# First-layer weight tiles from every fourth column, w_out in 8 KB rows, and w_in in three loads

## The chip, the cores and the metric

The kernel runs on one core of one Trainium2 chip. The core has five engines that run side by side: TensorE (PE in the profile, with its weight loads as PEld), VectorE (DVE), ScalarE (ACT), GpSimd (POOL) and SyncE (SP). Transfers between the chip's memory and the core's are issued here by SP and by POOL and carried out by the core's 16 DMA engines. The metric is the device time of one execution in microseconds; lower is better. Before the change the median of three runs is 308.4 us (308.37 to 308.42).

## The reference

Two steps follow each other. The first is attention with a window: 8 batches, 8 heads, 576 positions of 64 numbers, each position looking at those at most 32 away.

```python
scores = 1/sqrt(64) * q @ k.T                 # for each batch and head
scores = where(abs(i - j) <= 32, scores, -1e9)
attn   = exp(scores - max) / (sum + 1e-9)
x      = (attn @ v), heads side by side       # 4608 tokens x 512
```

The second is a layer pair on all 4608 tokens, with w_in of 512 x 2048 and w_out of 2048 x 512:

```python
h = x @ w_in
g = maximum(0.01 * h, h)
out = g @ w_out                               # 4608 x 512, float32
```

All inputs are float32; the kernel multiplies in bf16.

## The kernel before, in words

**Attention.** The work is cut into steps, one for a pair of heads and a stretch of tokens. In a step PE multiplies keys with queries (`score`, L429), ACT takes the exponential, POOL or DVE multiplies by the mask, PE forms the row sums (`row_sums`, L467) and the product with v (`product`, L517), and DVE inverts the sums and scales (`scaled`, L541), which leaves x transposed in `xT`: 128 rows (two heads) for each of four pairs p. Batches 0 and 1 are loaded plainly (`load_qk`, L68, on SP's queue), cast to bf16 (`cast_qk`, L286; the engines for q and k are its arguments) and transposed on PE (`transposes`, L327, matmuls at L340 and L344); later batches are transposed by the DMA engines.

**First layer.** The tokens are cut into groups `GROUPS` (L557), 288 tokens each for the first four. For a group g the first layer makes 16 tiles, f = 0 to 15; tile f is the product of columns 128 f to 128 f + 127 of w_in with xT, four matmuls that add up over the 512 inputs in chunks c of 128 (`h_mms`, L564, matmul at L567). The columns of w_in are the weights that PE loads ahead of each matmul. ACT applies the leaky ReLU and writes `gT[:, f]` (L572). w_in stands in one tile, `w_in_bf`, and is loaded by `load_w_in(f0, f1)` (L726) from POOL's queue, which also casts it to bf16: four loads of 512 columns, so that the weights of tiles 4 i to 4 i + 3 come with load i. A row of such a load is 512 floats, 2 KB, and there are 128 x 4 rows.

**Second layer.** For 128 tokens, 16 matmuls add up over the tiles f (L637; L653 in the first pair of output tiles, `o_pair`, L645, which goes through w_out in parts of four tiles f: (0,0), (0,1), (0,2), (1,0), and so on). `load_w_out(i)` (L729) brings rows 512 i to 512 i + 511 of w_out, again on POOL's queue with a cast: `w_out_bf[p, 4 i + c]` holds row 512 i + 128 c + p, so a row of the load is one row of w_out, 2 KB, and there are 128 x 4.

**Order.** The order is written out by hand; each engine takes its instructions in the order of the program, and an instruction that waits holds back those behind it on its engine. The part around the change is L733 to L860: the loads of w_in stand on POOL between casts and masks (L750, L767, L768, L785), those of w_out at L798, L804, L805 and L823. `h_first(0)` (L613) is a generator that makes tiles 0 to 3 of group 0 chunk by chunk: its first step takes four PSUM buffers, each further one issues the four matmuls of one chunk c, which needs the pair c of xT. Those steps stand between the attention work of steps 3 to 5 (L787 to L802). Then come tiles 4 to 15 of group 0 with the rest of the attention of batch 0 between them (L814), and group 1 (L846 to L859), into which `second_pair(p)` (L827) puts the transposes of batch 1, pair p, after tiles 7 and 11; pairs 2 and 3 come within `o_pair`. The q of batch 1 is cast on DVE, the k on POOL (L831, L838, L840, L859); on POOL the order is k of pair 0, two small clears, k of pair 1, three loads of v, a part of the band mask, k of pair 2, three loads of v, a mask, k of pair 3. The loads of q and k of batch 1 are issued on SP at L797, released by a one-element write on POOL (L75).

`row_sums_by_quarters(3)` (L485) makes the row sums of step 3 in another layout, with its matmuls at L490; `spread(3)` (L498) brings the inverse back.

The functions that the change touches, and those that call them:

Of the kernel before, what the change touches and what calls it, by code (L numbers as in the profile page):

```python
# [10 lines left out]
BF16 = mybir.dt.bfloat16  # L11
# [5 lines left out]
def kernel(  # L17
# [15 lines left out]
    nc = tc.nc  # L33
# [5 lines left out]
    DFF = moe_w_in.shape[1]  # L39
# [4 lines left out]
    DMC = DMODEL // 128  # L44
# [4 lines left out]
    const = ctx.enter_context(tc.tile_pool(name="const", bufs=1))  # L49
# [154 lines left out]
    for lo in (0, 64):  # L204
        w = win[lo:lo + 64]
        nc.gpsimd.affine_select(
            out=w, in_=w, compare_op=ALU.is_ge, fill=0.0,
# [3 lines left out]
            out=w, in_=w, compare_op=ALU.is_ge, fill=0.0,  # L211
# [53 lines left out]
    def clear_k(i, eng=nc.gpsimd):  # L265
# [7 lines left out]
        out=ps[:, 512:512 + HALF], in_=zero.to_broadcast([128, HALF]), func=AF.Copy,  # L273
# [4 lines left out]
    NEW_RING = 1024  # L278
    OLD = 8 * BY_DMA
    xT = const.tile([128, NPAIR, RING], BF16)  # L280
    w_in_bf = const.tile([128, DMC, DFF], BF16)
    w_out_bf = const.tile([128, FFC, DMODEL], BF16)

    def cast_qk(b, p, q_eng=nc.gpsimd, k_eng=nc.gpsimd):  # L286
        for eng, src, dst in ((q_eng, qf, qb), (k_eng, kf, kb)):
            if eng is None:
                continue
            if b == 0:  # L290
                to, tok = dst[:, p, 0:NB * D], src[b, p]
            else:
                to = dst[0:96, p].rearrange("p (c a d) -> p c a d", a=2, d=D)
                tok = src[b, p].rearrange("p a (c d) -> p c a d", d=D)
            if eng is nc.scalar:
                eng.activation(out=to, in_=tok, func=AF.Copy)
            else:
                eng.tensor_copy(out=to, in_=tok)  # L298
# [77 lines left out]
    def where(i):  # L376
        return i // 8, (i // 4) % 2, i % 4
# [6 lines left out]
    def score_blocks(i):  # L384
        p, bs = i % NPAIR, blocks_of(i)
        n = 2 * 64 * len(bs)
        lo = 512 * (i % 2)
        sc = ps[:, lo:lo + n].rearrange("p (a w c i) -> p a w c i", a=2, c=2, i=32)
        for w, (b, m) in enumerate(bs):
            tok = qz[b % 2][:, p, m // 3].rearrange("p a (c i) -> p a c i", c=2)  # L390
            at = 32 * (m % 3)
            nc.tensor.matmul(  # L392
                sc[:, :, w], kz[b % 2][:, p, 64 * m:64 * m + 128],
                tok[:, :, :, at:at + 32], start=True, stop=True,
            )
        e = attn.tile([128, 2 * HALF], BF16, name="e")
        nc.scalar.activation(out=e[:, 0:n], in_=ps[:, lo:lo + n], func=AF.Exp, scale=scale)  # L397
        pr = prob[:, i % NPROB].rearrange("p n i -> p (n i)")[:, 0:n]
        nc.gpsimd.tensor_mul(pr, e[:, 0:n], band.rearrange("p w c i -> p (w c i)")[:, 0:n])  # L399
        probs[i] = pr.rearrange("p (a w i) -> p a w i", a=2, i=64)  # L400
# [28 lines left out]
    def score(i, masked_by=nc.gpsimd):  # L429
        if i >= OLD:  # L430
            return score_blocks(i)
        b, hf, p = where(i)
        tok = qT[b][:, p, hf * HALF:hf * HALF + HALF]
        if b == 0:

            for a, n_, m in ((0, 0, 0), (1, 1, 0), (0, 0, 1), (1, 1, 1), (0, 0, 2),
                             (0, 1, 0), (1, 0, 0), (0, 1, 1), (1, 0, 1), (1, 0, 2)):
                blk, i0, n = WIN[hf][n_][m]
                r = slice(64 * a, 64 * a + 64)
                nc.tensor.matmul(  # L440
                    ps_v[r, n_, i0:i0 + n], first_keys[p][r, 64 * blk:64 * blk + 64],
                    tok[r, i0:i0 + n], start=True, stop=True,
                )
        else:
            for n_, blocks in enumerate(WIN[hf]):
                for blk, i0, n in blocks:
                    nc.tensor.matmul(  # L447
                        ps_v[:, n_, i0:i0 + n], kbd[b % 2][:, p, blk],
                        tok[:, i0:i0 + n], start=True, stop=True,
                    )  # L450
        e = attn.tile([128, 2 * HALF], BF16, name="e")
        nc.scalar.activation(out=e, in_=ps[:, P0:P0 + 2 * HALF], func=AF.Exp, scale=scale)  # L452
        pr = prob[:, i % NPROB]
        masked_by.tensor_mul(  # L454
            pr.rearrange("p n i -> p (n i)"), e, mask[hf].rearrange("p n i -> p (n i)"),
        )
        probs[i] = [pr, None, None]
# [27 lines left out]
    def row_sums_by_quarters(i):  # L485
        s = xps.tile([128, 512], FP32, name="s")
        pr = probs[i][0]
        for j in range(4):
            for n in range(2):
                nc.tensor.matmul(  # L490
                    s[:, 0:QUART], to_rows[:, 96 - 32 * j:224 - 32 * j],
                    pr[:, n, QUART * j:QUART * j + QUART],
                    start=(j == 0 and n == 0), stop=(j == 3 and n == 1),
                )
        nc.vector.reciprocal(quarters, s[:, 0:QUART])
        probs[i][2] = s

    def spread(i):  # L498
        s = probs[i][2]
        for j in range(4):  # L500
            nc.tensor.matmul(
                s[:, 128 + QUART * j:128 + QUART * j + QUART], from_rows[:, 128 * j:128 * j + 128],
                quarters, start=True, stop=True,
            )
        probs[i][2] = s[:, 128:128 + HALF]
# [6 lines left out]
    def sums(i):  # L512
        if probs[i][2] is None:
            row_sums(i)
            inverse(i)

    def product(i):  # L517

        b, hf, p = where(i)
        pr = probs[i][0]  # L520
        x = xps.tile([128, 512], FP32, name="x")[:, 0:HALF]
        parts = [(n_, *block) for n_ in range(2) for block in WIN[hf][n_]]
        for n_, blk, i0, n in parts:
            nc.tensor.matmul(  # L524
                x[:, i0:i0 + n], vbd[b % 2][:, p, blk, :], pr[:, n_, i0:i0 + n],
                start=(blk == parts[0][1]), stop=(blk == parts[-1][1]), skip_group_check=True,
            )
        if i in (1, 2, 3):

            to = kept[i] if i < 3 else recip.tile([128, HALF], FP32, name="r")  # L530
            nc.scalar.activation(out=to, in_=x, func=AF.Copy)
            x = to
        probs[i][1] = x
# [7 lines left out]
    def scaled(i):  # L541
        _, x, r = probs.pop(i)
        nc.vector.tensor_mul(place(i), x, r)
# [14 lines left out]
    t0, new = 0, NTOK - BY_DMA * S  # L558
    while t0 < new:
        n = 256 if t0 < 2048 else min(512, new - t0)  # L560
# [3 lines left out]
    def h_mms(g, f, h, cs):  # L564
        t0, n = GROUPS[g]
        for c in cs:
            nc.tensor.matmul(  # L567
                h[:, 0:n], w_in_bf[:, c, ts(f, 128)], xT[:, c, t0:t0 + n],
                start=(c == 0), stop=(c == DMC - 1),
            )  # L570

    def h_out(g, f, h):  # L572
        t0, n = GROUPS[g]
        to, h = gT[:, f, t0:t0 + n], h[:, 0:n]
        nc.scalar.activation(out=to, in_=h, func=AF.Prelu, alpha=0.01)  # L575
# [37 lines left out]
    def h_first(g):  # L613

        hs = [mmps.tile([128, 512], FP32, name="mm", tag="mm") for _ in range(4)]
        yield hs[0]
        for c in range(DMC):
            for f in range(4):
                h_mms(g, f, hs[f], (c,))
            if c == DMC - 1:  # L620
                for f in range(4):
                    h_out(g, f, hs[f])
            yield
# [38 lines left out]
    def warm_up(n, w=512):  # L662
        t = xps.tile([128, 512], FP32, name="x")
        for _ in range(n):
            nc.tensor.matmul(
                t[:, 0:w], idle[:, 0:128], idle[:, 0:w], start=True, stop=True,
                skip_group_check=True,
            )
# [52 lines left out]
        state["done"] += 1  # L721

    w_in_r = moe_w_in.rearrange("(c p) f -> p c f", p=128)
    w_out_r = moe_w_out.rearrange("(c p) f -> p c f", p=128)

    def load_w_in(f0, f1):  # L726
        nc.gpsimd.dma_start(out=w_in_bf[:, :, f0:f1], in_=w_in_r[:, :, f0:f1])  # L727

    def load_w_out(i):  # L729
        c = slice(4 * i, 4 * i + 4)  # L730
        nc.gpsimd.dma_start(out=w_out_bf[:, c, :], in_=w_out_r[:, c, :])

    first = transposes(0)  # L733

# [27 lines left out]
    next(first)  # L762
    next(first)
    warm_up(2)
    cast_qk(0, 3, nc.scalar, nc.gpsimd)
    load_cast_v(0, 3, (1,))
    load_w_in(512, 1024)  # L767
    load_w_in(1024, 1536)  # L768
    sums(1)
    score(2, masked_by=nc.vector)  # L770
    next(first)
# [7 lines left out]
    product(1)  # L779
    score(4)  # L780
    product(2)
    row_sums_by_quarters(3)
    scaled(1)
    scaled(2)
    load_w_in(1536, 2048)  # L785
    clear_on_act(kbd[1][:, 1])
    h0 = h_first(0)  # L787
    h = next(h0)
    next(h0)
    product(3)  # L790
    score(5)
    spread(3)
    scaled(3)
    next(h0)
# [79 lines left out]
    at, t = {1: 0.0}, 0.0  # L874
# [93 lines left out]
```

## Time and profile before

| | |
|---|---|
| median of the runs | 308.4 us (308.37, 308.40, 308.42) |
| the profiled execution | 308.76 us |
| its span, first to last instruction | 307.1 us |
| PE busy | 298.0 us, 97% |
| PEld, weight loads beside PE | 193.5 us, 63% |
| DVE, ACT, POOL busy | 72%, 66%, 66% |
| granted TensorE clock, mean | 1.000 |
| moved by the DMA engines | 48.31 MB in 121506 packets |

The profile is that of one execution. A span of an engine is the time in which it was busy; PEld overlaps PE. A row of the timeline gives start, duration, engine, line, operation, tiles and shape, and in brackets the idle time of the engine just before with what released it. The DMA view counts packets by queue: q0 is fed by POOL, q1 by SP. A load is split over the 16 DMA engines and has landed when the last of them is through.

### The profile page before, as it was taken

The numbers are of one execution on the slowest core, as the hardware profiler recorded it, in microseconds if no ns is written. First come the engines' busy times: TensorE is split into PE (matmuls) and PEld (weight loads), VectorE is DVE, ScalarE is ACT, GpSimd is POOL, SyncE is SP. The second block draws the span as 40 slices with busy tenths as digits, with TensorE's granted clock in tenths as the row PEclk, the third lists the DMA queues.
The fourth block names the chain that finished last, engine by engine and source line by source line (L and its number), as shares of the span: only waits on it lengthen the run. The fifth ranks groups of instructions, "written<-read, shape, count | busy, mean of one in ns | idle before, by whom it ended". The sixth has DMA issues, their size and how long they took to land.

```text
span 307.1 us, 6942 instructions
## 1 busy us (share of the span) xinstructions
PE 298.0 (97%) x2616; PEld 193.5 (63%) x2646; DVE 221.7 (72%) x302; ACT 204.1 (66%) x423; POOL 201.5 (66%) x258
## 2 busy tenths in 40 slices
PE   8799999999999999999999999999999999999996
PEld 3577855676757777676768685858555555444643
DVE  6879579597888987897799777898689766743000
ACT  7876964564946677685858585849589548843731
POOL 8989799867999996889577366579757533110000
PEclk9999999999999999999999999999999999999999
DMA  7999999998999999999969984994950110001002
GB/s 248 205 183 268 264 152 218 218 209 145 208 186 215 191 256 188 190 192 228 208 151 237 226 177 113 204 204 106 196 121 1 36 68 36 0 34 72 34 31 74
DMA packets 121506, 48.31 MB, mean 157 GB/s; under 512 B 96256, under 2 KB 115968, under 8 KB 121472
## 3 DMA queue, kind: packets, MB, share of 16 engines
q1 hardware_dynamic: 107776, 42.48, 67.9%
q0 software_dynamic: 13696, 5.38, 14.5%
q8 instruction: 21, 0.34, 0.5%
q14 instruction: 13, 0.11, 0.1%
HBM read 36.70 MB, written 9.44 MB: 150 GB/s over the span
## 4 chain that ended last, share of the span: by engine, by line
PE 86%; DMA 6%; POOL 5%; issue 1%; ACT 1%; POOLq 0%; ACTq 0%
PE mm L637 38%; PE mm L567 36%; DMA w_out_bf<-in_moe_w_out_dram 6%; PE ps L392 4%; PE s L410 2%; POOL set L147 2%; PE x L410 2%; PE mm L653 2%; POOL w_in_bf L727 1%; PE x L524 1%; POOL prob L454 1%; PE ps L447 0%; POOL kb L298 0%; ACT gT L575 0%; PE s L479 0%
## 5 line engine op out<-in xcount | busy, mean ns | idle before, releaser
L567 PE MATMUL mm<-xT,w_in_bf 128*128 128x256 bf16 (+3 forms) x956 | 133.5, 294 | 0.2
L637 PE MATMUL mm<-w_out_bf,gT 128*128 128x512 bf16 (+2 forms) x537 | 122.5, 373 | 1.3
L419 DVE RECIPROCAL r<-r 128x256 f32<-128x256 f32 (+1 forms) x56 | 95.0, 1696 | 34.3 <-ACT r L418 33.7
L567 PEld LDWEIGHTS <-w_in_bf 128*128 128x128 bf16 x960 | 91.4, 98 | 29.6
L399 POOL TENSOR_TENSOR prob<-e,band 128x512 bf16<-128x512 bf16 (+1 forms) x56 | 62.6, 1118 | 56.8 <-ACT e L397 55.6
L637 PEld LDWEIGHTS <-gT 128*128 128x128 bf16 x560 | 52.1, 98 | 54.1
L575 ACT ACTIVATE gT<-mm 128x288 bf16<-128x288 f32 (+2 forms) x112 | 49.9, 479 | 12.4 <-PE mm L567 9.9
L397 ACT ACTIVATE e<-ps 128x512 bf16<-128x512 f32 (+1 forms) x56 | 32.4, 579 | 27.6 <-PE ps L392 24.6
L642 ACT ACTIVATE o_sb<-mm 128x512 f32<-128x512 f32 (+2 forms) x35 | 20.5, 585 | 39.2 <-PE mm L637 38.9
L598 ACT ACTIVATE gT<-mm 128x512 bf16<-128x512 f32 x64 | 35.7, 596 | 5.3 <-PE mm L567 3.9
L509 DVE RECIPROCAL r<-s 128x288 f32<-128x288 f32 x13 | 25.4, 1957 | 3.8 <-PE s L476 2.4
L423 DVE TENSOR_TENSOR xT<-x,r 64x256 bf16<-64x256 f32 (+1 forms) x56 | 24.4, 436 | 3.7 <-PE mm L567 0.5
L298 POOL CAST kb<-kf 96x768 bf16<-96x768 f32 (+1 forms) x30 | 25.0, 832 | 3.0 <-DMA kf<-in_k_dram 2.5
L423 DVE TENSOR_TENSOR xT<-s,r 64x256 bf16<-64x256 f32 (+1 forms) x56 | 24.4, 435 | 3.3
L324 DVE COPY set<-kT 64x576 bf16<-64x576 bf16 x48 | 21.4, 446 | 1.7 <-DMA kT<-qb 0.8
L392 PEld LDWEIGHTS <-set 128*128 128x128 bf16 x216 | 16.8, 98 | 9.2
L392 PE MATMUL ps<-set 128*128 128x128 bf16 x216 | 21.2, 219 | 0.0
L303 POOL CAST set<-vbuf 128x640 bf16<-128x640 f32 x24 | 17.2, 717 | 4.5 <-DMA vbuf<-in_v_dram 2.8
L298 POOL CAST qb<-qf 96x768 bf16<-96x768 f32 x24 | 19.7, 820 | 0.1
L454 POOL TENSOR_TENSOR prob<-e,mask 128x576 bf16<-128x576 bf16 x13 | 16.5, 1275 | 2.9 <-ACT e L452 2.8
L410 PEld LDWEIGHTS <-set 128*128 128x128 bf16 x432 | 18.0, 98 | 0.5
L304 POOL CAST set<-vbuf 64x512 bf16<-64x512 f32 x24 | 14.6, 610 | 1.5
(104 smaller groups left out, 242.2 us busy)
## 6 DMA issues: line engine op xcount, KB each, us to landing
qf<-in_q_dram SPq DMA_DIRECT2D x32, 288.0 KB, 5.5
kf<-in_k_dram SPq DMA_DIRECT2D x32, 288.0 KB, 6.1
out_dram<-o_sb SPq DMA_DIRECT2D x35, 256.0 KB, 2.9
vbuf<-in_v_dram SPq DMA_DIRECT2D x15, 256.0 KB, 4.6
w_in_bf<-in_moe_w_in_dram POOLq DMA_DIRECT2D x4, 512.0 KB, 8.4
w_out_bf<-in_moe_w_out_dram POOLq DMA_DIRECT2D x4, 512.0 KB, 15.6
vbuf<-in_v_dram SPq DMA_DIRECT2D x10, 192.0 KB, 4.4
set<-in_v_dram POOLq DMA_DIRECT2D x16, 72.0 KB, 6.4
```

The source lines that it names most:

```text
L298: eng.tensor_copy(out=to, in_=tok)
L392: nc.tensor.matmul(sc[:, :, w], kz[b % 2][:, p, 64 * m:64 * m + 128], tok[:, :, :, at:at + 32], start=True, stop=True,)
L397: nc.scalar.activation(out=e[:, 0:n], in_=ps[:, lo:lo + n], func=AF.Exp, scale=scale)
L399: nc.gpsimd.tensor_mul(pr, e[:, 0:n], band.rearrange("p w c i -> p (w c i)")[:, 0:n])
L410: nc.tensor.matmul(x[:, a, w], vw[b % 2][:, p, m, a:a + 2].rearrange("p n d -> p (n d)"), pr[:, a, w], start=True, stop=True,)
L419: nc.vector.reciprocal(r[:, 0:n], r[:, 0:n])
L423: nc.vector.tensor_mul(xT[rows, p, t0:t0 + n].rearrange("p (w i c) -> p w c i", i=32, c=2), x[rows, a].rearrange("p (w c i) -> p w c i", c ...
L509: nc.vector.reciprocal(r, probs[i][2])
L567: nc.tensor.matmul(h[:, 0:n], w_in_bf[:, c, ts(f, 128)], xT[:, c, t0:t0 + n], start=(c == 0), stop=(c == DMC - 1),)
L575: nc.scalar.activation(out=to, in_=h, func=AF.Prelu, alpha=0.01)
L598: nc.scalar.activation(out=gT[:, f - 1:f + 1, t0:t0 + 256], in_=hh.rearrange("p (f t) -> p f t", f=2), func=AF.Prelu, alpha=0.01,)
L637: nc.tensor.matmul(o[:, lo:hi], gT[:, f, t0:t0 + 128], w_out_bf[:, f, lo:hi], start=(f == 0), stop=(f == FFC - 1),)
```

## The change

- A tile f of the first layer takes every fourth column: within a block of 512 columns n, tile 4 n + j takes columns 512 n + j, 512 n + j + 4, and so on, 128 of them. The weights of a matmul are then read with a step of four elements.
- To match that, `w_out_bf[p, 4 i + c]` holds row 512 i + 4 p + c, so that partition p takes four neighbouring rows of w_out, 8 KB in one piece, and a load has 128 rows in place of 512.
- w_in stands in three tiles of 512, 512 and 1024 columns. The third load brings the last 1024 columns at once, in rows of 4 KB; it stands where the load of columns 1024 to 1535 stood. The load at L785 goes. Tiles 8 to 15 now read the third tile.
- `h_first(0)` is begun earlier: its buffers and the first three matmuls of chunk 0 come before `row_sums_by_quarters(3)`; the fourth comes after `score(5)`.
- The cast of q, batch 0, pair 3, goes from ACT to DVE, where it stands behind the mask of step 1.

```diff
-    w_in_bf = const.tile([128, DMC, DFF], BF16)
+    w_in_parts = [const.tile([128, DMC, n], BF16, name=f"w_in{n_}") for n_, n in enumerate((512, 512, 1024))]
     w_out_bf = const.tile([128, FFC, DMODEL], BF16)
+
+    def w_in_cols(c, f):
+        n = min(f // 4, 2)
+        at = 128 * (f - 4 * n - f % 4)
+        return w_in_parts[n][:, c, at + f % 4:at + 512:4]
...
-                h[:, 0:n], w_in_bf[:, c, ts(f, 128)], xT[:, c, t0:t0 + n],
+                h[:, 0:n], w_in_cols(c, f), xT[:, c, t0:t0 + n],
...
             for f in range(4):
+                if c == 0 and f == 3:
+                    yield
                 h_mms(g, f, hs[f], (c,))
...
-    w_out_r = moe_w_out.rearrange("(c p) f -> p c f", p=128)
+    w_out_r = moe_w_out.rearrange("(i p c) f -> p i c f", p=128, c=4)
 
     def load_w_in(f0, f1):
-        nc.gpsimd.dma_start(out=w_in_bf[:, :, f0:f1], in_=w_in_r[:, :, f0:f1])
+        nc.gpsimd.dma_start(out=w_in_parts[min(f0 // 512, 2)], in_=w_in_r[:, :, f0:f1])
 
     def load_w_out(i):
         c = slice(4 * i, 4 * i + 4)
-        nc.gpsimd.dma_start(out=w_out_bf[:, c, :], in_=w_out_r[:, c, :])
+        nc.gpsimd.dma_start(out=w_out_bf[:, c, :], in_=w_out_r[:, i])
...
-    cast_qk(0, 3, nc.scalar, nc.gpsimd)
+    cast_qk(0, 3, nc.vector, nc.gpsimd)
     load_cast_v(0, 3, (1,))
     load_w_in(512, 1024)
-    load_w_in(1024, 1536)
+    load_w_in(1024, 2048)
...
     product(2)
+    h0 = h_first(0)
+    next(h0)
+    next(h0)
     row_sums_by_quarters(3)
     scaled(1)
     scaled(2)
-    load_w_in(1536, 2048)
     clear_on_act(kbd[1][:, 1])
-    h0 = h_first(0)
-    h = next(h0)
-    next(h0)
     product(3)
     score(5)
+    next(h0)
     spread(3)
     scaled(3)
     next(h0)
```

## The prediction, made before the run

> **What bounds the kernel now.** I read the page first: the share of each engine says which one the span hangs on.
>
> ```profile
> PE 298.0 (97%) x2616; PEld 193.5 (63%) x2646; DVE 221.7 (72%) x302; ACT 204.1 (66%) x423; POOL 201.5 (66%) x258
> ```
>
> PE is busy 97% of a span of 307.1 us, so what keeps PE waiting comes straight out of the time, and little waiting is left. The view of who waited for whom, for PE alone, shows what the change could remove:
>
> ```profile
> PE mm L653 <- DMA w_out_bf<-in_moe_w_out_dram: 0.6, 1, 0.6
> PE s L490 <- POOL prob L454: 0.6, 1, 0.6
> ```
>
> Columns are us in total, times, longest. Both are single waits of 0.6 us. The timeline of PE gives their places, and three places more that the change touches (start, duration, then in brackets the idle time before):
>
> ```profile
> 16.67 0.42 PE L490 MATMUL s<-prob,set 128*128 128x72 bf16 x8 [0.58 <-POOL prob L454]
> ...
> 24.44 0.65 PE L567 MATMUL mm<-xT,w_in_bf 128*128 128x288 bf16 x4
> ...
> 36.06 0.42 PE L344 MATMUL tp<-ident,kb 96*128 96x96 bf16 x6
> ...
> 38.77 0.42 PE L344 MATMUL tp<-ident,kb 96*128 96x96 bf16 x6
> ...
> 41.74 1.89 PE L653 MATMUL mm<-w_out_bf,gT 128*128 128x512 bf16 x8 [0.59 <-DMA w_out_bf<-in_moe_w_out_dram]
> ```
>
> The row at 24.44 is tile f=8 of the first group, counted from f=4 on in steps of four matmuls. The rows at 36.06 and 38.77 transpose the keys of batch 1, pairs 1 and 2. At all three PE does not wait: the data are just there. The chain of waits shows how long the awaited load had been under way, and two spacings on PE that I need below:
>
> ```profile
> 24.57 17.14 DMA w_out_bf<-in_moe_w_out_dram
> ...
> 57.44 1.47 PE mm L567 x12
> ...
> 73.92 0.23 PE x L410 x8
> ```
>
> The load of w_out issued at 24.57 lands 17.14 us later, at 41.71. So **up to 42 us the transfers decide**, and PE only just keeps behind them. After that PE is the bound to the end, and a delay at 42 us is a delay of the end.
>
> **Who shares the transfers.** Two queues feed the same 16 engines: POOL's (q0: v, w_in, w_out) and SP's (q1: q and k). In the DMA view for 25 to 37 us, when q0 carries w_out and q1 the queries and keys of batch 1, the columns are packets, MB, share:
>
> ```profile
> q0 software_dynamic: 1312, 1.31, 64.2%
> q1 hardware_dynamic: 1310, 1.86, 50.9%
> ```
>
> and for 46 to 47 us, when q0 carries v rows of 64 floats (256 B) and q1 mostly runs of 512 B:
>
> ```profile
> q0 software_dynamic: 432, 0.05, 85.8%
> q1 hardware_dynamic: 418, 0.20, 69.0%
> ```
>
> Both times the queues get as many packets each, though q0's are the larger in the one (2 KB read against 1.5 KB; q0 counts the bf16 bytes it writes, half of what it reads) and the smaller in the other. **The engines take turns by packet, not by byte.** The diff makes a w_out packet 8 KB.
>
> What the transfers of the present kernel meet, from the views of their issue lines (first the issue's start, then us from there to landing, min/median/max):
>
> ```profile
> L727 POOL DMA_DIRECT2D w_in_bf<-in_moe_w_in_dram x1: 808/808/808, 17.8 to 17.8; - x1
> ...
> DMA to landing us min/median/max: 8.9/8.9/8.9
> ```
>
> ```profile
> L731 POOL DMA_DIRECT2D w_out_bf<-in_moe_w_out_dram x2: 803/803/803, 20.3 to 23.8; - x2
> ...
> DMA to landing us min/median/max: 12.7/13.3/14.0
> ```
>
> ```profile
> L86 SPq DMA_DIRECT2D kf<-in_k_dram x1: 401/401/401, 21.8 to 21.8; - x1
> ...
> DMA to landing us min/median/max: 11.9/11.9/11.9
> ```
>
> So w_in's last quarter lands at 26.7, w_out's first two at 33.0 and 37.8, and the keys of pair 1 at 33.7. Landing means the last of the 16 engines.
>
> **The change, part by part.**
>
> *Three first tiles ahead.* They fill the wait before L490. In the chain twelve such matmuls take 1.47 us, 0.12 each, so three take 0.37 of the 0.58 us: a gain of 0.37, less some ends, 0.33. It reaches tile f=8 at 24.1 in place of 24.44.
>
> *The cast of q, pair 3, from ACT to DVE; one load fewer on POOL.* Both stand ahead of f=8, whose new wait (next) is longer than anything they could cost or bring: POOL's issues here take 0.8 us each, so bounds are -0.8 to +0.8 us. I take 0; without that cover it would be the 0.8.
>
> *Last two w_in chunks in one load.* Tile f=8 waited for the third quarter; now it waits for the third and fourth together. The queue is one line: bytes that were last at 26.7 stay last. What improves: 32 packets fewer on each engine, and 4 KB against q's 1.5 KB while the two share. The price of a packet comes from a stretch of 256 B packets (42 to 43 us) and one of 2304 B packets alone (3 to 8 us):
>
> ```profile
> q0 software_dynamic: 1076, 0.14, 216.1%
> ```
>
> ```profile
> q1 hardware_dynamic: 876, 1.78, 102.5%
> ```
>
> 16 engines over 1076 packets in 1 us is 14.9 ns each; over 876 in 5 us it is 91 ns. The difference, 76 ns for 2048 B, leaves about 5 ns that a packet costs whatever its size. 32 packets save 0.2 us; the larger share saves some 0.4. The load lands at 26.1 (bounds: 26.7, no saving; 25.2, if q starts so late that w_in runs alone). **PE waits at f=8 from 24.1 to 26.1; against before it is 1.7 us late.** Queued behind are all later tiles.
>
> *w_out's rows 8 KB long.* Each engine has 32 such packets in all, where it had 128, and 12 packets for each of the eight loads of q and k. In turns, the 48th packet of q/k, which ends the keys of pair 1, comes after all 32 of w_out. Before, when these keys landed (33.7), the last engine had done w_out's first 32 packets (33.0) and about 5 of the next: 37. Now 91 packets' worth more, 186 KB, goes ahead. That engine's rate: between 33.0 and 37.8 it moved 32 packets of 2 KB and 32 of 1.5 KB, 115 KB in 4.8 us, 23.9 KB/us. That is 7.8 us, and 128 packets fewer give 0.7 back: the keys land at 40.8. The last engine's lag may shrink with fewer packets; at 2 us less it is 38.8. I take 40.3, nearer the rate's row.
>
> w_out itself lands early: 32 turns of 9.7 KB at 23.9 KB/us are 13 us, from 26.1 to 39.1, before PE is there. The 0.59 us at 41.74 go.
>
> *What waits for the keys.* On POOL:
>
> ```profile
> 33.82 0.82 POOL L298 CAST kb<-kf 96x768 bf16<-96x768 f32 x1 [1.65 <-DMA kf<-in_k_dram]
> 34.59 2.27 POOL L147 DMA_DIRECT2D set<-in_v_dram  x3
> 36.84 0.54 POOL L226 MEMSET band<- 128x512 bf16 x1
> 37.62 0.82 POOL L298 CAST kb<-kf 96x768 bf16<-96x768 f32 x1 [0.23 <-DMA kf<-in_k_dram]
> ```
>
> The cast of pair 1 already sits on the landing. Behind it in POOL's order stand three loads of v, the band and the cast of pair 2, which ends at 38.44: 4.6 us from the first cast's start, 4.4 without the 0.23 of waiting. With the keys at 40.3 the cast of pair 2 ends at 44.7, and PE's transposes of pair 2, at 38.77 before, start there: **5.9 us late**. The waits at f=8 and at pair 1 lie inside that. Pairs 0 and 3 add nothing: 24 turns from about 25 us end near 35, where PE then is; pair 3 follows pair 2 as before. w_out's shorter issues on POOL (bounds 0 to 0.8 us each) are free, since POOL waits for keys.
>
> **Sum:** 5.9 - 0.6 = +5.3 us. On the profiled execution (308.76 us, its span 307.1 and 1.66 around it) that is 314.1; on the median of the runs, 308.4, it is **313.7**. Two costs have no row. Weight loads that take every fourth column: L567 starts a matmul each 0.12 us, while the eight of L410 in the chain load new weights each 0.03 us. A load may get some four times slower before it shows; 960 of them at 0.05 over the edge would be 48 us; I take 0. Idle PE may lose clock:
>
> ```profile
> 1.31 3.17 PE L665 MATMUL x<-prob 128*128 128x512 bf16 x7 [1.31 <-DVE prob L161]
> ```
>
> At the start seven matmuls of 512 columns take 3.17 us, 0.45 each, which is nearly twice the 288-column spacing scaled up (0.22). If a wait of 3 us put PE back there for as long again, that costs half of 3.2, 1.6 us, and 2.7 for a spell of 5.4. No wait that long is in this trace; I take 0 and keep 2.7 for the range.
>
> [...]
>
> **Rivals.**
>
> *The queues share by bytes above some size, or 8 KB are cut.* Then the keys keep near their times, and only f=8 remains: 1.7 - 0.6 = +1.1, 309.5; cut to 4 KB, some 41 of w_out's packets (82 of the old) precede the 48th of q/k in place of 37, 92 KB more or 3.9 us: keys at 37.6, the cast of pair 2 ends at 42.0, +3.2 - 0.6, 311.0. For it: no packet over 2.3 KB shares in this trace. Against: turns held at both size ratios.
>
> *Faster: long rows run so much better that w_in is early.* From f=8 to the wait at w_out PE has 16.7 us of work (41.74 - 0.59 - 24.44). The merged load decides at 25.0 us: landing there, with the keys in time, PE is at w_out at 41.7, where it was; landing at 24.1, both waits go, -0.33 - 0.59: 307.5. For it: the last engine's lag may come from many packets. Against: 5 ns a packet.
>
> *Strided weight loads become the bound:* 318 and more.
>
> **Chances.** Forecast 54% (its own range 311.7 to 316.5, the landing at 38.8 and the clock's 2.7 included); shared otherwise 19%; faster 20%; strided 7%. A measurement of this kernel can tell 0.2% (0.6 us) from no change. Faster by more 16% (the rest of that rival is too small), same 7%, slower 77%. The range runs from 307.8, which leaves out most of the faster case, to 317.0.
>
> **What would show it.** Right: in 25 to 37 us q0 and q1 with like counts of packets and q0 at 4 KB written each; PE idle before f=8, released by w_in; POOL idle for several us before the cast of pair 1; the keys landing near 40; no wait at w_out. Wrong: the keys at 34 (first rival), f=8 without a wait (second), or L567 spaced over 0.12 (third).

## The result: 313.9 us, and the profile after

The changed kernel takes **313.94 us** (median of six runs, 312.65 to 314.32), the kernel before 308.38 beside it: 1.0162 times as long, with a 95% interval of 1.014 to 1.0183. The profiled execution takes 314.32 us, 5.56 more than that of before, and its span is 312.6 us, 5.5 more. The forecast was 313.7 us by the median and 314.1 for the profiled execution.

Two lines of the page of the changed kernel, the first with the share of each engine, the second with packets, MB and share of POOL's queue over the whole span:

```profile
PE 299.9 (96%) x2646; PEld 205.8 (66%) x2646; DVE 223.6 (72%) x303; ACT 203.7 (65%) x422; POOL 200.4 (64%) x257
...
q0 software_dynamic: 11632, 5.38, 13.2%
```

PE is busy 1.9 us more, but the span is 5.5 longer, so most of the difference is waiting. q0 moves the same bytes in 2064 packets fewer. PE's waits in the changed kernel (us in total, times, longest):

```profile
PE tp L350 <- POOL kb L304: 4.0, 2, 3.0
PE mm L573 <- DMA w_in<-in_moe_w_in_dram: 1.7, 1, 1.7
```

The wait for w_out has gone. In its place stand one for w_in and two for the keys. Their places, in the timeline of PE:

```profile
25.93 0.68 PE L573 MATMUL mm<-xT,w_in 128*128 128x288 bf16 x4 [1.65 <-DMA w_in<-in_moe_w_in_dram]
...
40.66 0.43 PE L350 MATMUL tp<-ident,kb 96*128 96x96 bf16 x6 [2.98 <-POOL kb L304]
...
44.61 0.43 PE L350 MATMUL tp<-ident,kb 96*128 96x96 bf16 x6 [1.06 <-POOL kb L304]
```

These are tile f=8 and the transposes of the keys of pairs 1 and 2. Against the rows of before (24.44, 36.06, 38.77) PE is 1.49, 4.60 and 5.84 us late. What happens after that, from a row that is the same place in both kernels, a run of twelve first-layer matmuls; before:

```profile
127.23 1.47 PE L567 MATMUL mm<-xT,w_in_bf 128*128 128x256 bf16 x12
128.54 0.39 PE L392 MATMUL ps<-set 128*128 128x128 bf16 x4
128.76 0.40 PE L410 MATMUL s<-prob,set 128*128 128x64 bf16 x8
```

and after, with the one wait behind it:

```profile
132.36 1.47 PE L573 MATMUL mm<-xT,w_in 128*128 128x256 bf16 x12
133.67 0.27 PE L398 MATMUL ps<-set 128*128 128x128 bf16 x2
134.14 0.28 PE L398 MATMUL ps<-set 128*128 128x128 bf16 x2 [0.20 <-DMA set<-kb]
134.26 0.40 PE L416 MATMUL s<-prob,set 128*128 128x64 bf16 x8
```

At 127 us PE is 5.13 us late: 5.84 less the 0.59 of the wait at w_out that went, less 0.12 elsewhere. In the 85 us between, with some hundreds of strided weight loads, nothing is lost, and twelve matmuls take 1.47 us in both. Where the keys of a later batch come from a DMA transpose, at 134 us, another 0.4 is lost: the first two matmuls with this tile are still 5.13 us late (133.67 against 128.54), the next group is 5.50 late (134.26 against 128.76). These 5.5 us remain at the end.

Why the keys were late is in POOL's timeline of the changed kernel:

```profile
31.80 1.23 POOL L304 CAST kb<-kf 96x768 bf16<-96x768 f32 x1 [2.34 <-DMA kf<-in_k_dram]
...
39.79 0.82 POOL L304 CAST kb<-kf 96x768 bf16<-96x768 f32 x1 [6.15 <-DMA kf<-in_k_dram]
40.55 2.39 POOL L147 DMA_DIRECT2D set<-in_v_dram  x3
42.92 0.86 POOL L226 MEMSET band<- 128x512 bf16 x1
43.74 0.81 POOL L304 CAST kb<-kf 96x768 bf16<-96x768 f32 x1
```

POOL stands idle 6.15 us for the keys of pair 1, which land 6 us later than before, and only then gets through to the cast of pair 2, which ends at 44.55. The chain of waits names the load:

```profile
21.37 18.36 DMA kf<-in_k_dram
```

It was under way for 18.36 us. Where it was held up, the DMA view for 28 to 35 us shows (packets, MB, share):

```profile
q0 software_dynamic: 327, 1.20, 84.9%
q1 hardware_dynamic: 324, 0.46, 21.1%
```

q0's packets are now 3.7 KB written on average (1.20 MB in 327, from rows of 8 KB), 2.6 times the bytes counted for a packet of q1 (0.46 MB in 324), and still each queue gets one for one. q1 moves 46 packets a microsecond, where it moved 109 before (1310 in 12 us).

### The profile page after: what moved, and what is told of

Its sections match the earlier page's. It is cut to its first block, busy times and chain, and to the rows that moved or that the text cites. A ratio compares the mean times of both kernels' runs of the same rounds, so it can differ in the third digit from the quotient of the medians.

```text
span 312.6 us, 6971 instructions
## 1 busy us (share of the span) xinstructions
PE 299.9 (96%) x2646; PEld 205.8 (66%) x2646; DVE 223.6 (72%) x303; ACT 203.7 (65%) x422; POOL 200.4 (64%) x257
## 4 chain that ended last, share of the span: by engine, by line
PE 84%; DMA 7%; POOL 5%; ACT 2%; issue 1%; SPq 0%; POOLq 0%; ACTq 0%
PE mm L645 36%; PE mm L573 35%; DMA kf<-in_k_dram 6%; PE ps L398 4%; PE mm L661 2%; POOL set L147 2%; PE s L416 2%; PE x L416 2%; DMA set<-kb 1%; POOL kb L304 1%; PE x L530 1%; ACT e L458 1%; PE ps L453 1%; PE ps L446 0%; SPq L86 0%
## 5 line engine op out<-in xcount | busy, mean ns | idle before, releaser
L573 PE MATMUL mm<-xT,w_in 128*128 128x256 bf16 (+3 forms) x960 | 134.2, 294 | 1.7 <-DMA w_in<-in_moe_w_in_dram 1.7
L645 PE MATMUL mm<-w_out_bf,gT 128*128 128x512 bf16 (+2 forms) x560 | 124.6, 373 | 0.0
L573 PEld LDWEIGHTS <-w_in 128*128 128x128 bf16 x960 | 103.8, 114 | 20.2 <-DMA w_in<-in_moe_w_in_dram 2.1
```

The lines of the kernel that those rows point to most:

```text
L573: nc.tensor.matmul(h[:, 0:n], w_in_cols(c, f), xT[:, c, t0:t0 + n], start=(c == 0), stop=(c == DMC - 1),)
L645: nc.tensor.matmul(o[:, lo:hi], gT[:, f, t0:t0 + 128], w_out_bf[:, f, lo:hi], start=(f == 0), stop=(f == FFC - 1),)
```

## The experiments

Each kernel was run beside the kernel before, on the same chip; a ratio is to that one, with its 95% interval.

### The length of w_out's rows

**2 KB rows (e1).** The change, but each load of w_out is two loads of every second row, so that a packet is 2 KB again:

```diff
-        c = slice(4 * i, 4 * i + 4)
-        nc.gpsimd.dma_start(out=w_out_bf[:, c, :], in_=w_out_r[:, i])
+        for c in range(2):
+            nc.gpsimd.dma_start(out=w_out_bf[:, 4 * i + c:4 * i + 4:2, :], in_=w_out_r[:, i, c:4:2])
```

> The changed kernel, but each load of w_out is two loads of every second row, so that its packets are 2 KB again; layout, strided weights, merged w_in load and early tiles stay. Turns by packet: the keys of pair 1 land near 34 as before the change, PE does not wait for pairs 1 and 2; only the wait at f=8 (1.7 us) stays, less the wait at w_out: 309.5 us. If the strided weight loads or the merged load made the loss, it stays near 314.

Measured: 309.73 us against 308.56, ratio 1.0039 (1.002 to 1.0058). The DMA view for 25 to 37 us, and the largest wait of PE that stands in the part changed:

```profile
q0 software_dynamic: 1340, 1.30, 63.8%
q1 hardware_dynamic: 1333, 1.90, 51.1%
```

```profile
PE mm L573 <- DMA w_in<-in_moe_w_in_dram: 2.1, 1, 2.1
```

q1 has its 1.90 MB back (1.09 in the same 12 us with 8 KB rows), and PE waits nowhere for the keys of batch 1. Only the row length differs, and the number of issues, and 4.4 of the 5.56 us are gone. What is left fits the wait at f=8, 2.1 us, less the 0.59 at w_out. This is the run that carries the explanation.

**4 KB rows (e2).** The same with two neighbouring rows in each row of a load:

```diff
+        for c in (0, 2):
+            nc.gpsimd.dma_start(out=w_out_bf[:, 4 * i + c:4 * i + c + 2, :], in_=w_out_r[:, i, c:c + 2])
```

> As the run with 2 KB rows, with as many loads, but each of two neighbouring rows, so packets of 4 KB. Turns by packet: keys of pair 1 near 37.6, about 311.0 us, between the 2 KB and the 8 KB kernel. If the queues shared by bytes, packet size would not matter and this run would equal the one with 2 KB.

Measured: 313.33 us, ratio 1.0144 (1.0097 to 1.019): 2.3 us over what was expected. The casts of pairs 1 and 2 on POOL, and the granted clock (the number after POOL's busy time) in two stretches:

```profile
36.47 0.82 POOL L304 CAST kb<-kf 96x768 bf16<-96x768 f32 x1 [3.18 <-DMA kf<-in_k_dram]
...
41.96 0.82 POOL L304 CAST kb<-kf 96x768 bf16<-96x768 f32 x1 [1.63 <-DMA kf<-in_k_dram]
```

```profile
44.00:46.00 2.00, 2.00 (x11) 0.90 (x10) 1.64 (x5) 1.38 (x2) 2.00 (x3) 0.52 1.49 92
46.00:48.00 2.00, 2.00 (x7) 0.80 (x6) 0.97 (x6) 0.43 (x1) 2.00 (x3) 0.63 0.36 23
```

The keys of pair 1 come at 36.4, somewhat earlier than the 37.6 expected, but those of pair 2 come at 41.9 and hold POOL up a second time, so that PE transposes them at 42.83, 4.06 us late. At 4 KB w_out is spread over more turns and lasts longer: at 28 to 35 us q0 gets 0.97 MB through in 529 packets, to 560 of q1, where with 8 KB it is 1.20 MB in 327. The last two loads, issued at some 28 us, take 13.7 us by the median, so until about 42 (with 8 KB the last lands at 39.1), and the keys of pair 2 still share. The expectation had followed pair 1 alone. Then the granted clock falls to 0.52 and 0.63 for some 4 us (the last section comes back to that), and a row of PE that stands at 43.47 before stands at 48.47 here. Without the 0.59 at w_out the keys alone would make that 3.47 us late; it is 5.00, so some 1.5 us are the clock's. The fastest of the four runs, 310.64 us, is also the only one with a mean granted clock of 1.000; the others have 0.989 to 0.995 and 313.1 to 313.9 us. So the keys of pair 2 and the clock both stand in the 2.3 us; four runs do not tell how much belongs to each, and the one run at full clock is not above the 311.0 expected.

**8 KB rows, but later (e7).** The change with w_in in four loads, and with three of the four w_out loads behind the cast of the keys of pair 1 on POOL:

```diff
-    load_w_out(1)
-    load_w_out(2)
...
-            load_w_out(3)
...
+    for i in (1, 2, 3):
+        load_w_out(i)
```

> The changed kernel with w_in in four loads and with the last three loads of w_out moved on POOL behind the cast of the keys of pair 1. Turns by packet: q and k then share with one load of w_out only, all of them land by 35, the keys of pair 1 near 31, and w_out's loads run alone behind them and land near 37.5, 40 and 43, ahead of PE: no wait for keys or w_out, 307.5 us. If the loss is one of 8 KB packets as such, it stays at 311 or more.

Measured: 310.33 us against 308.76, ratio 1.0048 (1.0024 to 1.0072). Three views: POOL's cast of pair 1, PE's wait for w_out, and the DMA queue of q and k alone at 33 to 35 us:

```profile
32.93 0.82 POOL L302 CAST kb<-kf 96x768 bf16<-96x768 f32 x1 [0.52 <-DMA kf<-in_k_dram]
```

```profile
42.27 1.89 PE L659 MATMUL mm<-w_out_bf,gT 128*128 128x512 bf16 x8 [0.89 <-DMA w_out_bf<-in_moe_w_out_dram]
```

```profile
q1 hardware_dynamic: 319, 0.45, 105.1%
```

With the rows still 8 KB the keys of pair 1 come at 32.9 instead of 39.7, and some seven tenths of the loss go (e3, below, has the same parts with the loads in the old order and loses all of it). So for these seven tenths the long row does not cost by itself; it costs because it shares with the keys. It did not beat the kernel before, as I had expected it to: q and k alone run at only 160 packets a microsecond (0.45 MB in 2 us), so w_out, issued from 33.7 on, came 0.89 us late. That is only 0.3 more than in the kernel before; where the rest of the 1.6 us comes from stays open.

**The same order with 2 KB rows (e8).** The kernel before with the three early tiles, the cast on DVE, and the w_out loads moved as in e7:

```diff
-    load_w_out(1)
-    load_w_out(2)
...
-            load_w_out(3)
...
+    for i in (1, 2, 3):
+        load_w_out(i)
```

> The kernel before with the early tiles and the cast on DVE, and the last three loads of w_out (2 KB rows) moved on POOL behind the cast of the keys of pair 1. By the same reckoning the keys land near 31 and w_out's loads near 37, 39.5 and 42.5: no wait at w_out, 307.5 us. If the order of the loads has nothing to do with it: 308.4.

Measured: 311.0 us against 308.76, ratio 1.0077 (1.0048 to 1.0106), a miss, in part for the same reason. PE waits for w_out, and then for the loads of v that stand behind it on POOL's queue:

```profile
PE mm L655 <- DMA w_out_bf<-in_moe_w_out_dram: 0.9, 1, 0.9
...
PE x L524 <- DMA set<-in_v_dram: 0.8, 2, 0.5
```

Together that is 1.1 us more than the 0.59 of before, about half of the 2.2 us lost; the rest stays open.

### The merged load of w_in

**Merged load alone (e4).** The kernel before with a third tile of 1024 columns for w_in, loaded at once:

```diff
-    load_w_in(1024, 1536)
+    load_w_in(1024, 2048)
...
-    load_w_in(1536, 2048)
```

> The kernel before with one part of the change alone, the last two loads of w_in in one. PE waits at f=8 until about 26.3, 1.8 us later than before; 0.6 us come back at the wait for w_out: 309.5 us. If merging is free since the queue moves the same bytes: 308.4.

Measured: 310.66 us, ratio 1.0107 (1.0047 to 1.0167). The wait at f=8 is there:

```profile
26.05 0.66 PE L567 MATMUL mm<-xT,w_in 128*128 128x288 bf16 x4 [1.64 <-DMA w_in<-in_moe_w_in_dram]
```

1.64 us for a load that lands at 26.0; the wait at w_out has gone. Two of the four runs, with a mean granted clock of 1.000, take 309.65 and 309.73 us, which is the 309.5 expected; the two others take 311.59 at a clock of 0.994 and 313.64 at 0.988. A loss of 0.006 over 310 us is 1.9 us at full speed, which would account for these two. It is not shown that it does: the kernel before ran in 308.4 to 309.9 us at the same 0.994.

**The change without the merged load (e3).** The change with w_in in four tiles and four loads, the last where it was:

```diff
-    load_w_in(1024, 2048)
+    load_w_in(1024, 1536)
...
+    load_w_in(1536, 2048)
```

> The changed kernel with w_in in four loads again, the last at its old place on POOL; w_out stays in 8 KB rows. Turns by packet: the wait at f=8 goes, but the wait for the keys of pairs 1 and 2 takes its place, since the keys land near 40 all the same: 313.5 to 314 us. If the merged load is worth its own 1.7 us: 312.2.

Measured: 314.57 us, ratio 1.0199 (1.016 to 1.0237), not better than the whole change. The wait at f=8 is gone, and the queries and keys take all of it back. PE's rows, and the windows (span, busy PE, PEld, DVE, ACT, POOL, then the granted clock, DMA share, GB/s):

```profile
34.38 0.43 PE L348 MATMUL tp<-ident,kb 96*128 96x96 bf16 x6 [0.93 <-POOL kb L302]
38.64 0.43 PE L348 MATMUL tp<-ident,qb 96*128 96x96 bf16 x6 [1.87 <-DVE qb L302]
40.79 0.66 PE L348 MATMUL tp<-ident,kb 96*128 96x96 bf16 x6 [1.72 <-POOL kb L302]
```

```profile
36.00:38.00 2.00, 0.77 (x7) 0.45 (x4) 0.00 (x0) 1.06 (x3) 0.00 (x0) 1.00 1.03 278
38.00:40.00 2.00, 0.43 (x6) 0.28 (x6) 1.83 (x4) 0.65 (x1) 0.08 (x1) 0.89 1.11 242
40.00:42.00 2.00, 1.21 (x10) 0.94 (x11) 1.43 (x3) 0.51 (x1) 2.00 (x3) 0.50 0.73 175
```

So in the changed kernel the 1.65 us at f=8 lies inside the delay of the keys: a wait that is covered by a longer one behind it. In this execution PE's clock fell to 0.50 as well, until 46 us, and PE was 1.6 us later than in the changed kernel (the row at 43.47 before stands at 50.15 here and at 48.57 there). The clock is not why this kernel comes out no faster: its one run with a mean clock of 1.000 takes 314.11 us, little over the 313.5 to 314 expected.

### The weights from every fourth column

**Stride alone, in one tile (e5).** The kernel before with strided weight columns and w_out's rows to match, in 2 KB packets; w_in stays one tile:

```diff
-                h[:, 0:n], w_in_bf[:, c, ts(f, 128)], xT[:, c, t0:t0 + n],
+                h[:, 0:n], w_in_bf[:, c, 512 * (f // 4) + f % 4:512 * (f // 4) + 512:4], xT[:, c, t0:t0 + n],
```

> The kernel before with tiles of every fourth column and the matching layout of w_out, but w_out in 2 KB packets (two loads of every second row) and w_in in its four loads. If strided weight loads cost nothing: 308.4 us, L567 spaced as before. If they cost: more, spread over the whole span.

Measured: 317.93 us against 308.76, ratio 1.0287 (1.0259 to 1.0315), far from no change; but not by the weight loads. PE's largest wait:

```profile
PE mm L567 <- DMA w_in_bf<-in_moe_w_in_dram: 8.0, 1, 8.0
```

With a strided read, the first tiles waited for all four loads of w_in: the load that released them is the last one, issued at 17.6 us and landed at 26.8. This experiment said nothing of the weight loads; the next is its repair, in which w_in has a tile for each load and that wait is gone.

**Stride with four tiles, and its counterpart (e9, e11).** e9 is e5 with `w_in_parts` of 512 columns each; e11 is the kernel before with nothing but the split of each w_out load in two:

```diff
+            nc.gpsimd.dma_start(out=w_in_parts[f0 // 512], in_=w_in_r[:, :, f0:f1])
...
+                h[:, 0:n], w_in_parts[f // 4][:, c, f % 4:512:4], xT[:, c, t0:t0 + n],
```

```diff
+        for c in (4 * i, 4 * i + 1):
+            nc.gpsimd.dma_start(out=w_out_bf[:, c:4 * i + 4:2, :], in_=w_out_r[:, c:4 * i + 4:2, :])
```

> The kernel before with tiles of every fourth column, w_in in four tiles of its own (so that a weight load depends on its own load alone), w_out in the matching layout and 2 KB packets, two loads of every second row each. If strided weight loads cost nothing beside the matmuls, this equals the kernel with split w_out loads and no stride (next but one). If they do, L567's 960 matmuls stand further apart than 0.12 us.

> The kernel before, each load of w_out split into two of every second chunk of rows; layout and stride as before, packets 2 KB as before. The same packets in the same queue: 308.4 us, unless the last engine's lag is tied to the load's shape; then the wait at w_out goes and it is 307.9.

Measured: 309.83 us for e9 and 309.72 for e11, against 308.54: ratios 1.0039 (1.0016 to 1.0061) and 1.0037 (1.0007 to 1.0066). With and without the stride the time is the same, as closely as these intervals of some 0.3% can tell. The groups of the first layer (busy us, mean ns), e9 and then e11:

```profile
L567 PEld LDWEIGHTS <-w_in 128*128 128x128 bf16 x960 | 103.8, 114 | 18.1
L567 PE MATMUL mm<-xT,w_in 128*128 128x256 bf16 x512 | 59.4, 273 | 0.0
```

```profile
L567 PEld LDWEIGHTS <-w_in_bf 128*128 128x128 bf16 x960 | 91.4, 98 | 29.6
L567 PE MATMUL mm<-xT,w_in_bf 128*128 128x256 bf16 x512 | 59.3, 273 | 0.0
```

A strided weight load takes 114 ns where a plain one takes 98, and the matmuls take no longer: it lies beside them.

The split itself was not free, which I had expected it to be. In e11 PE waits for a mask, behind the row of POOL that holds it up:

```profile
28.75 0.41 PE L479 MATMUL s<-prob,ones_bd 128*128 128x288 bf16 x2 [0.70 <-POOL prob L454]
```

```profile
24.49 2.90 POOL L731 DMA_DIRECT2D w_out_bf<-in_moe_w_out_dram  x4
27.41 1.29 POOL L454 TENSOR_TENSOR prob<-e,mask 128x576 bf16<-128x576 bf16 x1
```

Four issues stand ahead of the mask on POOL where two stood, 0.72 us each, and PE waits 0.70 for it. This wait does not explain the 1.2 us, though: the 0.59 at w_out goes in return. PE is 0.55 us late at 44 us (44.02 against 43.47), of which 0.46 was there at 14.6 us already, before w_out is issued. A later wait for a mask, 0.48 us at 86.78, makes it 1.23. That the split causes this later wait is not shown.

**The same pair with the early tiles (e10, e12).** e10 is the change with 2 KB rows and w_in in four loads, that is, without both parts that looked costly; e12 is e11 with the early tiles and the cast on DVE, no stride. The edit of e12 beside e11:

```diff
+                if c == 0 and f == 3:
+                    yield
...
-    cast_qk(0, 3, nc.scalar, nc.gpsimd)
+    cast_qk(0, 3, nc.vector, nc.gpsimd)
...
+    h0 = h_first(0)
+    next(h0)
+    next(h0)
...
+    next(h0)
```

> The changed kernel without its two costly parts: w_out in 2 KB packets again (two loads of every second row) and w_in in four loads; stride, early tiles and the cast on DVE stay. No wait at f=8, keys near 32 to 34, w_out's third load near 40, before PE is there at 40.8: 307.6 us, faster than before by the wait at w_out and the 0.3 of the early tiles.

> As the run before, with the three early tiles and the cast on DVE. Differs from the changed kernel with 2 KB and four loads only by the stride: equal to it, near 307.6, if strided weight loads are free.

Measured: 309.77 us for e10, ratio 1.0023 (0.9997 to 1.0049), and 309.83 for e12, ratio 1.0037 (1.0013 to 1.0061). Again the stride makes no difference, and both miss the 307.6 expected. Nor does e10 gain anything on e1 (309.73), though the wait at f=8 is gone. The mask is not the reason here either. PE waits 0.69 us for it at 28.32, but nothing at w_out, and soon after it is within 0.12 us of the kernel before again; the first line is from before, the second from e10:

```profile
43.47 0.41 PE L479 MATMUL s<-prob,ones_bd 128*128 128x288 bf16 x2
43.59 0.41 PE L483 MATMUL s<-prob,ones_bd 128*128 128x288 bf16 x2
```

What e10 loses it loses later: it is 0.58 us late behind a wait for a mask at 86 us and 1.03 behind one for a transposed key set at 130 us. What the split of the loads has to do with these places stays open.

### The early tiles

**Early tiles and the cast (e6).** The kernel before with these two edits alone, as in the last diff.

> The kernel before with the three early tiles and the cast of q, pair 3, on DVE alone. My sum gave them 0.33 us up to f=8; but PE then only waits longer at w_out, whose third load lands at 41.7 either way: 308.4 us with a wait of 0.9 there. If the gain lasts: 308.05.

Measured: 308.76 us against 308.76, ratio 1.0008 (0.999 to 1.0026). The wait in front of L490, 0.58 us before, is shorter:

```profile
17.19 0.42 PE L490 MATMUL s<-prob,set 128*128 128x72 bf16 x8 [0.22 <-POOL prob L454]
```

The gain at this place is 0.36 us, and no gain in the time could be measured. The wait of 0.9 us that I had expected at w_out is not there: with w_out still in 2 KB rows, PE goes from 40.34 us on through twelve matmuls without a wait, the last eight of which, from some 41.2 on by their spacing, are those that had waited until 41.74. So the 0.59 us of the kernel before can go without a change to w_out.

No kernel tried was clearly faster than the one before.

## Why the prediction was right, step by step

**Early tiles, cast and load on POOL (0.33, and 0).** In the changed kernel PE was ready for f=8 at 25.93 - 1.65 = 24.28; 24.1 was forecast. Alone the two edits change nothing that can be measured (e6).

**The merged load (lands 26.1, PE 1.7 us late).** The matmuls behind it started at 25.93, 1.49 us late. Alone it costs some 1.1 us at full clock (e4), what was given for the rival that left only this cost. In the change it is covered by the keys (e3), as the sum had it. The price of 5 ns a packet, from which the 26.1 comes in part, does not hold for q1: rows of 1.5 KB alone took 16 engines x 2 us over 329 packets, 97 ns each (last section), no less than the 91 ns of the larger rows in the prediction. The terms worked out with it, 0.2 and 0.7 us, are small.

**Turns by packet (keys of pair 1 at 40.3).** This is the step on which the forecast stood. The counts are 327 to 324 with packets 2.6 times as large; POOL's cast shows the keys at 39.7. w_out was forecast for 39.1. Its four loads took 13.3 us at the longest from issue to landing, in the view of its issue line:

```profile
L739 POOL DMA_DIRECT2D w_out_bf<-in_moe_w_out_dram x4: 538/600/607, 19.9 to 25.8; - x4
...
DMA to landing us min/median/max: 8.6/10.0/13.3
```

and that is the last, issued at 25.8: 39.1. Undoing this step alone takes 4.4 of the 5.56 us back (e1), and so do seven tenths of them without shortening a row (e7). One sign that I had named came out only in part: over all of 25 to 37 us the counts are 516 to 767, not alike. At 26 to 28 w_out fell back (73 to 214), and from 36 on it was through on most engines (40 to 484 at 36 to 39). So it is the last engines that set both landings, at 39.1 and 39.7. Why w_out fell back at 26 to 28 stays open, and since the sum had it take its turns without a break from 26.1 on, that 39.1 came out to the tenth is luck.

**The cast of pair 2 (ends at 44.7).** It ended at 44.55, by two errors that nearly cancel, which is luck: the keys came 0.6 us earlier than forecast, and from the first cast to the end of the second POOL took 44.55 - 39.79 = 4.76 us instead of 4.4, above all because the band's clear took 0.86 us instead of 0.54.

**The sum (5.9 - 0.6).** 5.84 us late at pair 2, and the 0.59 at w_out gone, though e6 shows that this wait can go by itself. The 0.4 us at 134 us were not in the sum. They arise between two neighbouring groups of matmuls, at the wait for a transposed key set, the only one behind 46 us that PE's waits show (the row has 0.20 idle, since the ends of matmuls are modelled). Why this set came late stays open. The forecast's own range, 311.7 to 316.5, is not quite what its two terms give: 1.5 us less for keys at 38.8 is 312.2, and 2.7 more for the clock is 316.4.

**Strided weights (0).** Right: 114 against 98 ns, and no time that could be measured (e9 beside e11, e10 beside e12).

**Clock (0, up to 2.7 kept).** Right for the profiled execution, whose mean granted clock is 0.999 in spite of a wait of 2.98 us. Two of the six runs have 0.995 and 0.989 and are no slower than the others. That it could have been otherwise e3 shows, whose profiled execution is 1.6 us later than that of the changed kernel, with the clock at 0.50 from 40 to 46 us. The seven matmuls from which the 2.7 is reckoned do not show it: they take 0.45 us each, but the granted clock recorded there, at 1 to 5 us of the kernel before, is 1.00.

**Rivals.** Sharing by bytes is refuted by the counts (327 to 324 packets for 1.20 to 0.46 MB); rows cut to 4 KB by the 3.7 KB written per packet (1.20 MB in 327). The price for 4 KB, 311.0, had left out that the keys of pair 2 then share to the end: in e2 PE was 4.06 us late at them, where 3.2 was reckoned. For the faster case w_in had to land at 25.0, and it came at 25.9.

## What to carry to other kernels

When two queues feed the same DMA engines and take turns by packet, a longer row on one of them is a larger share for it (here, at 25 to 37 us, q0 wrote 1.86 MB to q1's 1.09 with rows of 8 KB, and 1.31 to 1.86 with 2 KB): ask whose data is needed first before making a row longer, and count the packets of both queues that lie ahead of the load that something waits for. Where a transfer arrives early, look for the one that paid for it: here w_out's third load landed at 35.1 instead of 41.7 us, and the keys of pair 1 at 39.7 instead of 33.7. And a wait taken away helps only if no longer one stands behind it: without the wait at f=8 the time was the same.

## What the runs showed of the hardware

**A turn is not a whole load.** Over 16 engines the rows of a load of q or k make 12 packets on each; those of a load of w_out make 8 in the change and in e2, 16 in e1, 32 before. If a whole load had its turn, the counts would stand as 8, 8, 16 and 32 to 12. At 28 to 35 us they stand as 327 to 324 in the change, 529 to 560 in e2, 779 to 779 in e1 and 766 to 764 before. Turns of equal size, of one packet or of several, would give such counts; turns as long as a load's rows would not.

**q and k alone move fewer bytes than the two queues together.** When w_out was through, q and k had the engines of the changed kernel to themselves at 38 to 40 us:

```profile
q1 hardware_dynamic: 329, 0.47, 110.4%
```

0.47 MB in 2 us is some 235 GB/s. At 28 to 35 us the two queues together read 2.40 MB for w_out (twice what q0 wrote) and 0.46 for q and k, 409 GB/s. So putting these transfers one after the other (e7, e8) costs bandwidth, which I had not counted. It is not that q1 alone can do no more: at 3 to 8 us of the kernel before it moved 1.78 MB in 5 us, 356 GB/s, mostly in rows of 2.3 KB. That is 175 packets a microsecond, here it is 165, so the number of rows looks like the limit rather than their bytes; no run changes the rows of q and k alone.

**The clock can fall without one long wait.** In e3 PE's longest wait was 1.87 us, and the granted clock fell to 0.50 for some 6 us; in the changed kernel a wait of 2.98 us left it at 1.00 up to 54 us. In e2 the longest wait was 2.09 us, and the clock was at 0.52 and 0.63 from 44 to 48 us. In e3 PE was busy 0.77 and 0.43 us in two neighbouring stretches of 2 us, from 36 us on. In e5, where PE stood idle for 7.95 us from 19 us on, the clock was 0.98 at 20 to 22 us and 0.50 from 22, so it fell after some 3 us. The idle time of several waits close together, added up, does not explain it either: e2 lost the clock after 4 us in which PE was busy 1.86 us (0.74 and 1.12), and the changed kernel kept it through 4 us with 1.34 (0.00 and 1.34, from 38 us on). What decides it stays open.

**Issuing a load with fewer rows is cheaper.** POOL took 0.54 to 0.61 us to issue a load of w_out with 128 rows (the row of L739 above), and 0.75 to 0.80 with 512 (747 to 803 ns at L731 before).
